# Linear attention and two MLPs: pass 4 takes blocks 1 to 8 in pairs, 512 columns wide, and VectorE turns the finished tiles

## The chip, the core and the metric

The kernel runs on 1 core of one Trainium2 chip. The metric is device time in microseconds (us), the median of several executions.

## What is computed

```python
kv = np.einsum('bhsd,bhse->bhde', k, v)              # batch 8, 8 heads, 576 tokens, head size 64
out = np.einsum('bhsd,bhde->bhse', q, kv)
rms = np.sqrt(np.mean(out * out, axis=-1, keepdims=True) + 1e-06)
x = out / rms * g_norm                               # then as 4608 tokens x 512
h = x @ w_in_1                                       # 512 x 2048
x = np.maximum(0.01 * h, h) @ w_out_1                # 2048 x 512
h = np.maximum(x @ w_in_2, 0.0)
out = (h * h) @ w_out_2                              # 4608 x 512, float32
```

## The kernel before, in words

The 4608 tokens are nine blocks of 512 (`TB`), and the two MLPs are four passes over them. Pass 1 computes attention and the first product with `w_in_1` (`gemm1`). Pass 2 multiplies with `w_out_1` (phase 0, `ph = 0`), pass 3 with `w_in_2` (`first`), pass 4 with `w_out_2` (`ph = 1`).

Every float32 operand of a matmul is split into a high and a low part (names ending in h and l), and three products hh, hl, lh are summed. ScalarE writes the high part (a copy to the rounded type), VectorE subtracts it and writes the low part.

Passes 2 to 4 multiply 2x2 blocks of matrices with seven products instead of eight, in Winograd's form (`PRODUCTS`): S1 to S4 are sums of quarters of the left operand A, T1 to T4 of the right operand B, and the products are added into the results C11, C22, C21 and C12. `ORDER` and `ORDER2` are the orders in which the products run. The 2048 values that are summed over come in four groups n of 512 (`NQ`), and within n in two halves c.

There are two ways to run a product with a `w_out`.

- `second_pass` and `second`: one block at a time, group by group and in it product by product, 256 columns wide. VectorE and ScalarE prepare the sums and the parts of the activations for each group (`prep`, `sum_op`, `hi_op`, `lo_op`). In phase 0 the weights are the left operand and the result stands with its features on the partitions. In phase 1 the activations are the left operand and the result stands with its tokens on the partitions, as `out` wants it.
- `pairs_pass` and `pair_second`: two blocks at a time, one the B11, B21 half and the other the B12, B22 half, product by product and in it group by group. A unit is one product and one group: 12 matmuls of 512 columns, weights on the left. `pair_load` loads a quarter (tile `dB`), `pair_sum` makes the T sums, `pair_hi` and `pair_lo` the parts (`dop_B..`, `dop_T..`; the digit in the name is the group n), and `adder` adds a finished PSUM tile (`dps`) to earlier sums into `du` or `do_C`.

Before the change pass 2 runs block 0 with `second_pass` and blocks 1 to 8 with `pairs_pass`; pass 4 runs all nine blocks with `second_pass`, in the order 7, 8, 0, 5, 6, 3, 4, 1, 2. So the weights of `w_out_1` are stored as A quarters and S sums, those of `w_out_2` as B quarters and T sums (`LEFT`).

The order of the work is written out as numbers: `at_slot(t, step)` puts a step at a place on a scale of slots, and the steps are emitted sorted by it. `tick` is called once for each product and group; a store that was put down by `store` is issued by SyncE (SP) two ticks later. All loads stand in the same SP queue, and a load waits there until the buffer it takes (46 of them, `NBIG`) is free. Weights come in 28 tiles, fetched as buffers come free; those of the second half are split on arrival (`split_loaded`). Finished tiles that wait for their store share 5 buffers (`hp`). PSUM's 8 banks are handed out in turn (`next_bank`), and `bank_swap` exchanges some at the start of pass 4, where the last products of pass 3 and the first of pass 4 alternate on TensorE.

Of the kernel before, what the change touches and what calls it, by code (L numbers as in the profile page):

```python
# [10 lines left out]
F32 = mybir.dt.float32  # L11
# [3 lines left out]
ALU = mybir.AluOpType  # L15
# [3 lines left out]
def tile_linear_attention_two_mlps(  # L19
# [111 lines left out]
    def pre_split(w, n):  # L131
# [3 lines left out]
         for j in range(NB if ph else 1)]  # L135
# [3 lines left out]
        j: [[dram.tile([P, 2, TB], F32, name=f"h{k}_{j}_{n}") for n in range(NQ)] for k in range(2)]  # L139
        for j in range(1, NB)  # L140
# [112 lines left out]
    LEFT = {(0, 1): 0, (1, 0): 0, (1, 1): 1}  # L253
# [16 lines left out]
    def store(out, in_, *slots):  # L270
        stores.append([out, in_, slots, 0])

    def tick():
# [14 lines left out]
    def sum_w2(w, n, name):  # L288
# [9 lines left out]
        w: [PRODUCTS[p][LEFT[w]] for p in (ORDER if w[0] else ORDER2)] for w in LEFT  # L298
# [429 lines left out]
    def operand(kind, b, name):  # L728
# [7 lines left out]
        if kind == 1:  # L736
            i, j = j, i
# [95 lines left out]
    def square(u, z, pairs, name):  # L833
# [22 lines left out]
    def second(ph, gg, x, free):  # L856
        j, n = gg
        tick()
        pr = (ORDER if ph else ORDER2)[x]
        if ph and n == 0 and pr == 1 and j == SETS[-1][0]:  # L860
            k = bank_n[0]
            bank_swap.update({(k + x) % 8: (k + y) % 8 for x, y in ((1, 2), (2, 3), (3, 1))})
# [3 lines left out]
        gname = PRODUCTS[pr][1 - ph]  # L866
        g = op_t[ph, gg, gname][0]
        last = n == NQ - 1
        for c in range(2):
            w = w2((ph, 1), 2 * n + c, x)  # L870
            for t in range(2):
                for y, (gh, wh) in enumerate(((0, 0), (0, 1), (1, 0))):
                    if ph == 0:
                        a, b = w[:, gh, t, :], g[wh][:, c, :]
                    else:
                        a, b = g[gh][:, c, t * P:(t + 1) * P], w[:, wh].rearrange("p c f -> p (c f)")
                    nc.tensor.matmul(  # L877
                        out=ps[:, t], lhsT=a, rhs=b,
# [11 lines left out]
        if pr == (1 if ph else 6):  # L890
# [6 lines left out]
        if pr in outs:  # L897
# [12 lines left out]
    d_done = set()  # L910
    PLACE = {"T3": "B12", "T2": "B11", "T4": "T3", "T1": "T2"}
# [417 lines left out]
```

## Time and profile before

| | |
|---|---|
| median of 3 runs | 1569.1 us (1567.08 to 1569.54) |
| the profiled execution | 1569.42 us, of which its span on the core 1567.6 us |
| TensorE busy | 1553.0 us, 9260 matmuls |
| VectorE, ScalarE busy | 1171.3 us, 808.1 us |
| granted TensorE clock | full in all slices |
| mean DMA rate | 202 GB/s |

The page gives the busy time of each engine (PE is TensorE's matmuls, PEld its weight loads, DVE VectorE, ACT ScalarE, SPq SyncE's queue of DMAs), the chain of work that ended last, the costliest groups of instructions and the DMAs. The trace is asked for parts of it: a timeline of an engine, busy times in stretches, the chain in order of time, one line's instructions. L877 is the matmul of `second`, L958 that of `pair_second`, L810 that of `first`, L789 is `adder`.

### The profile page before, as it was taken

What the parts mean: (1) busy time and instruction counts of PE and PEld (TensorE: products, weight loads), DVE (VectorE), ACT (ScalarE), POOL (GpSimd) and SP (SyncE); (2) the same over time, 40 slices, a digit from 0 to 9 for tenths busy, and PEclk for the clock granted to TensorE, in tenths of its full rate; (3) what the DMA queues carried; (4) which work ended last, traced back from release to release, by engine and by line L of the source; (5) the groups of instructions that cost most, each with busy time, mean ns of one, the idle gap of its engine ahead of it and who ended that gap; (6) DMA issues with size and microseconds to landing.
All of it is one profiled execution on the core that took longest, in us unless ns stands there. A gap on an engine that the chain in (4) does not pass through costs nothing.

```text
span 1567.6 us, 24422 instructions
## 1 busy us (share of the span) xinstructions
PE 1553.0 (99%) x9260; PEld 1357.0 (87%) x9260; DVE 1171.3 (75%) x1752; ACT 808.1 (52%) x1341; POOL 7.2 (0%) x16
## 2 busy tenths in 40 slices
PE   7999999999999999999999999999999999999999
PEld 5788888888888988888888888889888999999998
DVE  5866776777774988787776777767777887777776
ACT  5866666666665534344443544546446444443442
POOL 0000000000000000000000000000000000000000
PEclk9999999999999999999999999999999999999999
DMA  9978788889569737373746444655579444433332
GB/s 241 287 207 290 255 313 285 296 285 334 215 215 313 252 108 232 99 233 98 237 172 225 159 164 162 188 182 185 165 228 346 153 134 135 131 125 124 122 124 78
DMA packets 221525, 317.24 MB, mean 202 GB/s; under 512 B 52448, under 2 KB 150240, under 8 KB 221408
## 3 DMA queue, kind: packets, MB, share of 16 engines
q1 hardware_dynamic: 220048, 315.13, 61.7%
q8 instruction: 73, 1.20, 0.3%
q10 hardware_dynamic: 1360, 0.56, 0.1%
q14 instruction: 44, 0.36, 0.1%
HBM read 191.89 MB, written 123.73 MB: 201 GB/s over the span
## 4 chain that ended last, share of the span: by engine, by line
PE 97%; DMA 1%; DVE 1%; ACT 1%; issue 0%; SPq 0%; DVEq 0%
PE ps L877 25%; PE hps L675 25%; PE dps L958 19%; PE aps L810 12%; PE bps L810 9%; PE kvps L502 1%; PE qtps L554 1%; PE ops L581 1%; PE ops L580 1%; PE ops L579 1%; DMA w<-w 0%; PE ssps L609 0%; PE ssps L603 0%; DMA g<-h_C 0%; DMA v_raw<-in_v_dram 0%; PE ssps L601 0%
## 5 line engine op out<-in xcount | busy, mean ns | idle before, releaser
L675 PE MATMUL hps<-xh,w 128*128 128x512 f32 x1152 | 378.7, 396 | 2.1 <-ACT xh L632 1.3
L675 PEld LDWEIGHTS hps<-xh,w 128*128 128x128 f32 x1152 | 216.1, 188 | 49.8 <-DVE w L245 1.9
L675 PE MATMUL hps<-xl,w 128*128 128x512 f32 x576 | 224.6, 390 | 0.5 <-DVE xl L633 0.5
L675 PEld LDWEIGHTS hps<-xl,w 128*128 128x128 f32 x576 | 108.3, 188 | 22.7 <-issue 1.0
L687 ACT ACTIVATE h<-hps 128x512 f32<-128x512 f32 x144 | 85.0, 593 | 24.2 <-issue 10.2
L926 DVE TENSOR_TENSOR dB<-dB,dB 128x1024 f32<-128x1024 f32 x64 | 78.2, 1222 | 1.1 <-DMA dB<-h 0.2
L789 DVE TENSOR_TENSOR h_C<-aps,u 128x512 f32<-128x512 f32 x72 | 49.6, 688 | 38.8 <-PE aps L810 38.5
L789 DVE TENSOR_TENSOR u<-bps,p 128x512 f32<-128x512 f32 x72 | 49.5, 687 | 27.7 <-ACT p L820 17.9
L389 DVE TENSOR_TENSOR w<-w 128x512 fp32r<-128x512 f32 x56 | 37.8, 687 | 35.4 <-ACT w L388 35.4
L820 ACT ACTIVATE p<-aps 128x512 f32<-128x512 f32 x36 | 21.3, 592 | 74.9 <-PE aps L810 74.9
L562 DVE TENSOR_TENSOR qhl<-qtps,qhl 128x512 fp32r<-128x512 f32 x32 | 22.1, 691 | 46.2 <-ACT qhl L561 43.6
L810 PE MATMUL aps<-op_B21h,w 128*128 128x512 f32 (+1 forms) x160 | 51.8, 373 | 0.7 <-ACT p L820 0.7
L212 DVE SCALAR_TENSOR_TENSOR w_raw<-w_raw 128x512 uint32<-128x512 uint32 x64 | 44.1, 688 | 9.8 <-ACT w_raw L211 9.4
L810 PE MATMUL aps<-op_B22h,w 128*128 128x512 f32 (+1 forms) x160 | 51.1, 368 | 0.0
L810 PE MATMUL bps<-op_T4h,w 128*128 128x512 f32 (+1 forms) x160 | 51.1, 368 | 0.0
L810 PE MATMUL bps<-op_T3h,w 128*128 128x512 f32 (+1 forms) x160 | 51.0, 368 | 0.0
L810 PE MATMUL aps<-op_B11h,w 128*128 128x512 f32 (+1 forms) x160 | 51.0, 368 | 0.0
L810 PE MATMUL aps<-op_T1h,w 128*128 128x512 f32 (+1 forms) x160 | 51.0, 368 | 0.0
L810 PE MATMUL bps<-op_T2h,w 128*128 128x512 f32 (+1 forms) x160 | 51.0, 368 | 0.0
L620 DVE TENSOR_TENSOR sqo<-sqo,y 128x512 f32<-128x512 f32 x32 | 22.1, 692 | 35.2 <-ACT y L618 34.9
L827 ACT ACTIVATE h_C<-aps 128x512 f32<-128x512 f32 x36 | 21.5, 597 | 51.6 <-issue 32.9
L561 ACT ACTIVATE qhl<-qtps 128x512 fp32r<-128x512 f32 x32 | 19.1, 597 | 52.2 <-PE qtps L554 52.2
(908 smaller groups left out, 4032.9 us busy)
## 6 DMA issues: line engine op xcount, KB each, us to landing
g_raw<-g SPq DMA_DIRECT2D x80, 512.0 KB, 5.6
dB<-h SPq DMA_DIRECT2D x80, 512.0 KB, 4.0
g<-h_C SPq DMA_DIRECT2D x144, 256.0 KB, 2.4
h<-h SPq DMA_DIRECT2D x128, 256.0 KB, 4.6
w_raw<-in_moe_w_in_dram SPq DMA_DIRECT2D x32, 512.0 KB, 7.0
w_raw<-in_moe_w_out_dram SPq DMA_DIRECT2D x32, 512.0 KB, 6.8
x_raw<-x SPq DMA_DIRECT2D x32, 512.0 KB, 6.1
w<-w SPq DMA_DIRECT2D x56, 256.0 KB, 4.9
```

The costliest lines, as they stand in the source:

```text
L212: nc.vector.scalar_tensor_tensor(out=lower, in0=upper, scalar=0x80000000, in1=lower, op0=ALU.bitwise_and, op1=ALU.bitwise_or,)
L389: nc.vector.tensor_tensor(out=by_h[:, :, 1], in0=src[:, :, 1], in1=src[:, :, 0], op=ALU.subtract)
L562: nc.vector.tensor_tensor(out=t[:, 1], in0=ps, in1=f32(t[:, 0]), op=ALU.subtract)
L620: (nc.gpsimd if i == 1 else nc.vector).tensor_tensor(out=osb, in0=osb, in1=y, op=ALU.mult)
L675: nc.tensor.matmul(out=ps, lhsT=w[:, wh, c * P:(c + 1) * P], rhs=x_t[j][xh, c // 2][0][:, c % 2, :], start=(c == 0 and y == 0), stop=(c == ...
L687: nc.scalar.activation(out=h, in_=h_ps.pop((j, m)), func=AF.Prelu, alpha=0.01)
L789: nc.vector.tensor_tensor(out=t, in0=x, in1=y, op=ALU.add)
L810: nc.tensor.matmul(out=ps[:, p], lhsT=w[:, wh, c, :], rhs=t[xh][:, c, :], start=(fresh and p == 0 and c == 0 and y == 0), stop=(p == len(p ...
L827: nc.scalar.activation(out=h, in_=ps, func=AF.Relu)
L877: nc.tensor.matmul(out=ps[:, t], lhsT=a, rhs=b, start=(n == 0 and c == 0 and t == 0 and y == 0), stop=(last and c == 1 and y == 2), skip_g ...
L926: nc.vector.tensor_tensor(out=to[0], in0=d_t[z, x, n][0], in1=d_t[z, y, n][0], op=op)
L958: nc.tensor.matmul(out=ps[t], lhsT=w[:, wh, t, :], rhs=ops[gh][:, c, :], start=(n == 0 and at == pr and c == 0 and y == 0), stop=(last and ...
```

## The change

- Pass 4 runs block 0 with `second_pass` and then the pairs (7, 8), (5, 6), (3, 4), (1, 2) with `pairs_pass`, as pass 2 does; the functions of the pairs get the phase as an argument. The weights of `w_out_2` are prepared as A quarters and S sums.
- Pass 3 stores the blocks 1 to 8 in the layout that the pairs load (`h_d[1, ...]`).
- The results of pass 4 now stand with their features on the partitions. VectorE turns each finished tile in 32x32 blocks (`turned`), and `store_out` writes a turned tile in 4 DMAs, one for each 32 features, whose runs in `out` are 32 floats. For C11 of a pair the transpose reads PSUM and takes the place of ScalarE's copy. The last two tiles' DMAs are issued by SP and ScalarE in turn.
- In the last group of each product of a pair, in both passes, the first half of the tile (`t = 0`) is finished before the second.
- The first two steps of pass 3 stand 2.5 slots earlier, and `bank_swap` at the start of pass 4 exchanges two triples of banks.

The diff, without the renaming of keys and arguments in the pair functions:

```diff
-    LEFT = {(0, 1): 0, (1, 0): 0, (1, 1): 1}
+    LEFT = {(0, 1): 0, (1, 0): 0, (1, 1): 0}
...
-            store(
-                g_d[1][SETS[z][t]][n][:, i, :, cp * U:(cp + 1) * U],
-                h.rearrange("p c (t u) -> p (c t) u", t=2),
-            )
+            store(h_d[1, SETS[z][t]][i][n][:, cp], h.rearrange("p c t -> p (c t)"))
...
-        pr = (ORDER if ph else ORDER2)[x]
-        if ph and n == 0 and pr == 1 and j == SETS[-1][0]:
+        pr = ORDER2[x]
+        if ph and n == 0 and pr == 6:
             k = bank_n[0]
-            bank_swap.update({(k + x) % 8: (k + y) % 8 for x, y in ((1, 2), (2, 3), (3, 1))})
+            bank_swap.update({(k + x) % 8: (k + y) % 8 for x, y in ((1, 2), (2, 3), (3, 1), (4, 5), (5, 6), (6, 4))})
...
             if ph == 0:
-                to = x2_d[j][2 * i:2 * i + 2].rearrange("c p t -> p c t")[:, :, o * U:(o + 1) * U]
+                store(x2_d[j][2 * i:2 * i + 2].rearrange("c p t -> p c t")[:, :, o * U:(o + 1) * U], e)
             else:
-                t0 = j * TB + i * U
-                to = out[t0:t0 + U, o * U:(o + 1) * U].rearrange("(c p) f -> p c f", p=P)
-            store(to, e)
+                et = turned(f"t{j}_{name}", e)
+                for t in range(2):
+                    store_out(j * TB + o * U, 2 * i + t, et[:, t], U)
+
+    R = 32
+
+    def turned(name, src):
+        t = hp.tile(list(src.shape), F32, tag="h", name=name)
+        flat = (lambda x: x) if len(src.shape) == 2 else lambda x: x.rearrange("p c t -> p (c t)")
+        nc.vector.transpose(flat(t), flat(src))
+        return t
+
+    def store_out(t0, f, t, n, last=False):
+        for b in range(P // R):
+            f0 = f * P + b * R
+            store(
+                out[t0:t0 + n, f0:f0 + R].rearrange("(c r) f -> r c f", r=R),
+                t[b * R:(b + 1) * R].rearrange("r (c f) -> r c f", f=R),
+                by=nc.scalar if last and b % 2 else nc.sync,
+            )
...
-        for c in range(2):
-            w = w2((0, 1), 2 * n + c, x)
-            for t in range(2):
-                for y, (wh, gh) in enumerate(((0, 0), (0, 1), (1, 0))):
+        ws = [w2((ph, 1), 2 * n + c, x) for c in range(2)]
+        for c, t in sorted(((c, t) for c in range(2) for t in range(2)), key=lambda ct: ct[1] if last else ct[0]):
+            for y, (wh, gh) in enumerate(((0, 0), (0, 1), (1, 0))):
...
-                if pr == 2:
+                if pr == 2 and ph:
+                    e = ps[t]
+                elif pr == 2:
...
-                store(x2_d[SETS[z][o]][2 * i + t], e)
+                if ph:
+                    et = turned(f"dt{z}_{name}{t}", e)
+                    store_out(SETS[z][o] * TB, 2 * i + t, et, TB, pr == 3 and z == Z_ORDER[1][-1])
+                else:
+                    store(x2_d[SETS[z][o]][2 * i + t], e)
...
-                    at_slot(at0, "f", u, z, mine, n, free)
+                    at_slot(at0 if u or n > 1 else at0 - 2.5, "f", u, z, mine, n, free)
...
-        second_pass(t3, 1, [j for half, z in insts if half for j in SETS[z]])
+        pairs_pass(second_pass(t3, 1, [0]), 1)
```

Three places in the order of the program show it. On TensorE, after the first block of pass 4 (`ps_7`, `ps_8` are PSUM tiles of blocks 7 and 8, the digit behind them the product; `w_11` are tiles of the weights), there stood before:

```order
L877 MATMUL ps_7_3_11424<-w_11_24_11416,op_(7, 3)_S_11678 128x256 x6
L877 MATMUL ps_7_3_11424<-w_11_27_11471,op_(7, 3)_S_11678 128x256 x6
L877 MATMUL ps_8_6_11840<-w_11_0_10834,op_(8, 0)_S_11702 128x256 x6
L877 MATMUL ps_8_6_11840<-w_11_3_10905,op_(8, 0)_S_11702 128x256 x6
L877 MATMUL ps_8_1_11857<-w_11_0_10834,op_(8, 0)_A_11716 128x256 x6
L877 MATMUL ps_8_1_11857<-w_11_4_10928,op_(8, 0)_A_11716 128x256 x6
```

and now, after block 0:

```order
L870 MATMUL ps_0_4_11433<-op_(0, 3)_T_11695,w_11_23_11420 128x256 x6
L870 MATMUL ps_0_4_11433<-op_(0, 3)_T_11695,w_11_27_11503 128x256 x6
L870 MATMUL ps_0_3_11456<-op_(0, 3)_B_11726,w_11_24_11448 128x256 x6
L870 MATMUL ps_0_3_11456<-op_(0, 3)_B_11726,w_11_27_11503 128x256 x6
L968 MATMUL dps_1_0_11897<-dop_B_0h,w_11_0_10866 128x512
L968 MATMUL dps_1_0_11897<-dop_B_0l,w_11_0_10866 128x512
```

The next block's groups of 256 columns gave way to the pair's units of 512.

On VectorE, where a block of pass 4 ends (`o_C` and `do_C` are finished tiles, `sS` sums, `op` and `dop` operands), there stood before:

```order
L789 TENSOR_TENSOR o_C_14722<-ps_4_2_14350,p_14_14701 128x512
L769 TENSOR_TENSOR op_(1, 0)_A_14705<-g_raw_1_0_1_14553,op_(1, 0)_A_14705 128x512
L789 TENSOR_TENSOR u_14_14739<-ps_4_7_14366,u_14_14703 128x512
L769 TENSOR_TENSOR op_(1, 0)_S_14725<-sS_1_(1, 0)_14708,op_(1, 0)_S_14725 128x512
L769 TENSOR_TENSOR op_(1, 0)_S_14741<-sS_1_(1, 0)_14664,op_(1, 0)_S_14741 128x512
L789 TENSOR_TENSOR u_14_14758<-ps_4_5_14383,u_14_14703 128x512
L789 TENSOR_TENSOR o_C_14760<-ps_4_5_14383,u_14_14739 128x512
```

and now, from C21 of the pair (7, 8) to the first operands of the pair (5, 6):

```order
L789 TENSOR_TENSOR do_C_12380<-dps_4_0_12302,du_140_12124 128x512
L906 STREAM_TRANSPOSE dt_C_12382<-do_C_12380 128x512
L789 TENSOR_TENSOR do_C_12384<-dps_4_1_12303,du_141_12126 128x512
L906 STREAM_TRANSPOSE dt_C_12386<-do_C_12384 128x512
L952 TENSOR_TENSOR dop_B_2l<-dB_14_2_12132,dop_B_2h 128x1024
L937 TENSOR_TENSOR dB_13_2_12230<-dB_13_2_12320,dB_13_2_12230 128x1024
L952 TENSOR_TENSOR dop_B_3l<-dB_14_3_12151,dop_B_3h 128x1024
```

The transposes stand between the adders and the next low parts.

On SP, in the second pair of pass 4, the stores of a C (here C22) now stand between the loads of the next pair's quarter B22 (`dB22_12`), 8 DMAs in a row:

```order
L931 DMA dB22_12_2_12906<-h1_1_4_2_235 128x1024
L281 DMA out_0_dram<-dt3_C220_12876 32x16x32 x4
L281 DMA out_0_dram<-dt3_C221_12880 32x16x32 x4
L931 DMA dB22_12_3_12933<-h1_1_4_3_236 128x1024
L931 DMA dB11_12_0_12952<-h1_0_3_0_221 128x1024
```

Before, a C of pass 4 left in one DMA.

## Rows read from the trace of the kernel before

**Rows 1.** The page, part 1: busy us (share of the span) xinstructions

```profile
PE 1553.0 (99%) x9260; PEld 1357.0 (87%) x9260; DVE 1171.3 (75%) x1752; ACT 808.1 (52%) x1341; POOL 7.2 (0%) x16
```

**Rows 2.** The chain in order of time, its long pieces: start us, us, what

```profile
506.85 40.46 PE ps L877 x336
547.31 304.67 PE dps L958 x1344
...
1208.12 355.68 PE ps L877 x2964
```

**Rows 3.** Stretches, a pair and a block: us, busy by engine, PEclk, DMA share, GB/s

```profile
699.50:775.60 76.10, 76.10 (x337) 63.06 (x336) 58.51 (x55) 32.23 (x33) 0.00 (x0) 1.00 0.52 166
1251.00:1291.30 40.30, 40.30 (x338) 40.30 (x337) 33.35 (x54) 16.97 (x30) 0.00 (x0) 1.00 0.43 145
```

**Rows 4.** TensorE's timeline at two seams: start us, us, what [idle before <-releaser]

```profile
855.53 0.38 PE L810 MATMUL aps<-op_B21h,w 128*128 128x256 f32 x1 [0.69 <-ACT p L820]
...
1205.03 1.70 PE L877 MATMUL ps<-w,op_(7, 0)_S 128*128 128x256 f32 x12 [1.24 <-DVE h_C L789]
```

**Rows 5.** The timeline of VectorE and TensorE in pass 4's first block

```profile
1226.36 0.69 DVE L389 TENSOR_TENSOR w<-w 128x512 fp32r<-128x512 f32 x1 [1.28 <-ACT w L388]
1226.96 0.69 DVE L769 TENSOR_TENSOR op_(7, 3)_S<-sS_(7, 3)_11577,op_(7, 3)_S 128x512 fp32r<-128x512 f32 x1
...
1241.07 1.60 PE L877 MATMUL ps<-w,op_(8, 0)_S 128*128 128x256 f32 x12
```

**Rows 6.** The page, part 5, VectorE: xcount | busy us, mean ns | idle before

```profile
L926 DVE TENSOR_TENSOR dB<-dB,dB 128x1024 f32<-128x1024 f32 x64 | 78.2, 1222 | 1.1 <-DMA dB<-h 0.2
...
L389 DVE TENSOR_TENSOR w<-w 128x512 fp32r<-128x512 f32 x56 | 37.8, 687 | 35.4 <-ACT w L388 35.4
```

**Rows 7.** Line 591, a one-source copy: ns min/median/max, first and last start us

```profile
L591 DVE CAST sqs<-sqo x28: 419/426/429, 86.7 to 447.2; 128x512 fp32r<-128x512 f32 x28
```

**Rows 8.** VectorE's timeline at two seams between pairs of pass 2

```profile
699.01 1.37 DVE L789 TENSOR_TENSOR do_C<-dps,du 128x512 f32<-128x512 f32 x2 [0.18 <-PE dps L958]
700.30 1.22 DVE L941 TENSOR_TENSOR dop_B_2l<-dB,dop_B_2h 128x1024 fp32r<-128x1024 f32 x1
...
759.60 1.23 DVE L941 TENSOR_TENSOR dop_B_0l<-dB,dop_B_0h 128x1024 fp32r<-128x1024 f32 x1 [1.33 <-PE dps L958]
...
764.34 1.32 DVE L789 TENSOR_TENSOR do_C<-dps,du 128x512 f32<-128x512 f32 x2
...
767.85 1.22 DVE L941 TENSOR_TENSOR dop_B_3l<-dB,dop_B_3h 128x1024 fp32r<-128x1024 f32 x1
768.98 1.22 DVE L926 TENSOR_TENSOR dB<-dB,dB 128x1024 f32<-128x1024 f32 x1
```

**Rows 9.** TensorE's timeline behind the first of these seams

```profile
704.93 0.39 PE L958 MATMUL dps<-dop_B_2h,w 128*128 128x512 f32 x1
...
707.65 0.39 PE L958 MATMUL dps<-dop_B_3h,w 128*128 128x512 f32 x1
```

**Rows 10.** DMA queues, 20 to 60 us: packets, MB, share of 16 engines

```profile
DMA packets 16165, 10.51 MB, mean 263 GB/s; under 512 B 5993, under 2 KB 16161, under 8 KB 16161
...
q1 hardware_dynamic: 16161, 10.46, 109.1%
```

**Rows 11.** DMA queues, 1240 to 1540 us

```profile
q1 hardware_dynamic: 17179, 39.68, 40.2%
```

**Rows 12.** SP's timeline at the second seam: stores of C22, then loads

```profile
756.99 0.86 SPq L279 DMA_DIRECT2D x<-do_C  x2
759.33 7.81 SPq L920 DMA_DIRECT2D dB<-h  x4
```

**Rows 13.** Loads of q, tile q_raw: issue ns min/median/max, first and last start

```profile
L542 SPq DMA_DIRECT2D q_raw<-in_q_dram x126: 533/598/1675, 0.7 to 390.4; - x126
```

**Rows 14.** The page, part 6: xcount, KB each, us to landing

```profile
dB<-h SPq DMA_DIRECT2D x80, 512.0 KB, 4.0
```

**Rows 15.** The chain's last piece: start us, us, what

```profile
1563.83 0.69 DVE o_C L789
```

More of the change, by code (lines that the diff above doesn't have):

```diff
@@ L134, in tile_linear_attention_two_mlps @@
         [[dram.tile([P, 2, 2, TB], F32, name=f"g{ph}_{j}_{n}") for n in range(NQ)]
-         for j in range(NB if ph else 1)]
+         for j in range(1)]
         for ph in range(2)
@@ L138, in tile_linear_attention_two_mlps @@
     h_d = {
-        j: [[dram.tile([P, 2, TB], F32, name=f"h{k}_{j}_{n}") for n in range(NQ)] for k in range(2)]
-        for j in range(1, NB)
+        (ph, j): [
+            [dram.tile([P, 2, TB], F32, name=f"h{ph}_{k}_{j}_{n}") for n in range(NQ)] for k in range(2)
+        ]
+        for ph in range(2) for j in range(1, NB)
     }
@@ L268, in tile_linear_attention_two_mlps, with store @@
     stores = []
-    def store(out, in_, *slots):
-        stores.append([out, in_, slots, 0])
+    def store(out, in_, *slots, by=nc.sync):
+        stores.append([out, in_, slots, 0, by])
     def tick():
@@ L277, in tick @@
         while stores and stores[0][3] > 1:
-            to, src, slots, _ = stores.pop(0)
-            nc.sync.dma_start(out=to, in_=src)
+            to, src, slots, _, by = stores.pop(0)
+            by.dma_start(out=to, in_=src)
             give_big(*slots)
@@ L297, in tile_linear_attention_two_mlps @@
     w_names = {
-        w: [PRODUCTS[p][LEFT[w]] for p in (ORDER if w[0] else ORDER2)] for w in LEFT
+        w: [PRODUCTS[p][LEFT[w]] for p in (ORDER2 if w[1] else ORDER)] for w in LEFT
     }
@@ L872, in second @@
                 for y, (gh, wh) in enumerate(((0, 0), (0, 1), (1, 0))):
[L873 to L876, printed above, removed]
                     nc.tensor.matmul(
-                        out=ps[:, t], lhsT=a, rhs=b,
+                        out=ps[:, t], lhsT=w[:, gh, t, :], rhs=g[wh][:, c, :],
                         start=(n == 0 and c == 0 and t == 0 and y == 0),
@@ L889, in second @@
             u_t["p1"] = p1
-        if pr == (1 if ph else 6):
+        if pr == 6:
             u_t["u2"] = adder("gl", f"u2_{ph}{j}", bank[6], u_t["p1"])
@@ L910, in tile_linear_attention_two_mlps @@
     d_done = set()
+    Z_ORDER = (list(range(1, len(SETS))), list(range(len(SETS) - 1, 0, -1)))
     PLACE = {"T3": "B12", "T2": "B11", "T4": "T3", "T1": "T2"}
@@ L1109, in second_pass @@
             gs = [(j, n) for j in blocks for n in range(NQ)]
-            steps = prep("TS"[ph], not ph)
+            steps = prep("T", True)
             for x, gg in enumerate(gs):
@@ L1121, in second_pass, with pairs_pass @@
                     at_slot(at0 + n + 0.1, "s2", ph, gg, n, True)
-                if ph and gg[0] == blocks[-1]:
-                    at_slot(at0 + NPR, "wd", (ph, 1), gg[1])
             return t0 + NPR * len(gs)
         at_slot(0, "lag", 5)
-        def pairs_pass(t0):
-            for z in range(1, len(SETS)):
+        def pairs_pass(t0, ph):
+            for z in Z_ORDER[ph]:
                 def at_unit(w, *st):
```

92 lines of the change are left out of this document (46 added, 46 removed).

## The prediction

> **What bounds the kernel now.** I read the page's first part, then the chain of work that ended last in order of time, then the busy time of the engines stretch by stretch. TensorE is busy 1553.0 of 1567.6 us [rows 1], so only what shortens or interrupts its own stream counts. The chain shows the stages in that stream [rows 2]: block 0 of pass 2, 336 matmuls 256 columns wide in 40.46 us, 120.4 ns each; the pairs of pass 2, 1344 matmuls 512 wide in 304.67 us, 226.7 ns each; pass 4 without its first dozens of matmuls, 2964 matmuls 256 wide in 355.68 us, 120.0 ns each. A column costs 0.469 ns in pass 4 and 0.443 ns in the pairs. The stretches say why [rows 3]: in a block of pass 4 the weight loads are busy 40.30 of 40.30 us, so each 256-column product waits for its load; in a pair they are busy 63.06 of 76.10 us, and the 512 columns cover them. Pass 4 is bound by weight loads and pass 2's pairs are not.
>
> **Matmuls.** Pass 4 now runs 9 x 336 = 3024 matmuls of 256 columns. After, block 0 keeps its 336, and 2688 of 256 become 1344 of 512: 2688 x 120.0 ns = 322.6 us against the 304.67 us which the same program of four pairs took in pass 2: **-17.9 us**. All of it lies on TensorE, which sets the end. The exchange of A sums for B sums in the weights of pass 4 keeps the number and size of the operations of pass 1: nothing. So does the new layout of pass 3's stores: the same bytes in half the packets, beside pass 3's matmuls.
>
> **The seams.** Between pass 3 and pass 4 TensorE waits 1.24 us, for a VectorE adder that empties a PSUM bank [rows 4]. After, product 5 goes to the bank of an older, already emptied tile and that bank to product 3, two to three products later: -1.24 us, if nothing else is late. Between passes 2 and 3 TensorE waits 0.69 us for ScalarE's copy of product 1 [rows 4], because product 2 follows on the same bank. The two still stand side by side after the change; only product 6 has moved: nothing.
>
> Something else is late: VectorE at the first pair. No earlier row shows this mix, so I add up the new order from the last split of weights, which starts at 1226.36; the next operation starts at 1226.96 [rows 5]. From there to the end of the low part of B11's third quarter stand 18 operations of 512 elements and 7 of 1024; they follow each other every 0.60 and 1.13 us [rows 5, 8]: 18.7 us, so 1245.7. TensorE wants it two units of 2.72 us after the start of the pair: at 1246.5 with today's start of 1241.07 [rows 5], at 1245.3 if the 1.24 us are gained. So most of that gain is handed back: **+1.0 us**, with bounds of 0 and 3.5 (VectorE today idles 1.4 us in that stretch, and two more units hang on it).
>
> **VectorE.** A pair takes it 58.5 of 76.1 us [rows 3]. The trace has no 32x32 transpose. Nearest rows: for 512 elements a one-source copy takes 426 ns [rows 7] and a two-source operation 687 ns, and one of 1024 elements, as if each element passed twice, 1222 ns [rows 6]. I take 0.69, as for all other work on this shape; 8 of them bring a pair to 64.0 of 76.1 us. Their place matters more. Where a pair ends, VectorE works from 759.60 on without a gap [rows 8], and the transposes of C21 (2) and C12 (2) fall there. C22's two, 1.2 us, are taken up by the gap of 1.33 us before that. C21's push the rest back by 1.2 us: the adders of C12, free at 699.01 - 0.18 = 698.83 now, start at 700.0, four operations take 2.4 us, and the low part of B11's third quarter ends at 703.7. TensorE wants it at 704.93 and the fourth at 707.65 [rows 9]: 1.2 us of slack, today 3.4. So 0.69 us costs **nothing** and 1.22 us would cost 0.9 us at each of three seams.
>
> **DMA and SP.** A finished tile of 128 x 512 leaves in 4 DMAs of 64 KB, 2048 packets of 128 B in all; a pair has 8 tiles, so 16384 packets, 1024 for each of the 16 DMA engines. The trace has no such packet. Two stretches give the price of mean sizes: 1.091 x 16 x 40 us / 16161 = 43.2 ns at 647 B [rows 10], 0.402 x 16 x 300 us / 17179 = 112.3 ns at 2310 B [rows 11]. The line through both gives 21.6 ns at 128 B, my estimate; bounds are 8.5 (in proportion to bytes) and 43.2 (a packet costs what it cost at 647 B). A pair of pass 2 keeps the engines busy 0.52 of the time [rows 3], 39.6 us; less 64 packets of 2 KB for the x stores (101 ns each by the line, 6.5 us) and plus 1024 x 21.6 ns it is 55 of 76.1 us: it fits. SP issues 2 stores per quarter of a result now, in 0.86 us [rows 12], and 8 after; loads of up to 512 packets take it 598 ns each [rows 13], so 4.8 us. Behind the stores of C22 waits the fourth load of B22. It now leaves at 759.33, after at 757.0 + 4.8 = 761.8, and with the 4.0 us of such loads [rows 14] lands at 765.8, behind the burst (256 packets per engine, 5.5 us) perhaps at 767; the sum that needs it starts at 768.98 [rows 8]. Behind C21's stores waits the fourth load of B11, with more room. A new wait: C21's second adder takes the buffer of C22's first turned tile and needs its four DMAs landed: 757.0 + 4 x 0.6 + 4.0 = 763.4, against 764.34 and two operations of 0.6 [rows 8], 765.5. All of this is covered: **nothing**, and cover of 2 us is thin.
>
> **The tail.** Now the last adder ends at 1563.83 + 0.69 = 1564.52 [rows 15], 3.1 us before the span's end. After, the first half tile ends 1.36 us earlier and keeps VectorE until the last adder; that one needs a transpose (0.69) and the second of two issues on its queue (0.6), and 8 DMAs, 256 packets per engine, must pass: by the chain of the second half +1.5 us, by the packets at 21.6 ns about +3. I take **+2.5**, bounds +1.5 and +8.5 (43 ns).
>
> **Sum.** The profiled execution took 1569.42 us, span 1567.6, 0.3 above the median of 1569.1. 1569.4 - 17.9 - 1.2 + 1.0 + 2.5 = **1553.8 us**; its own range is 1551.5 to 1558.
>
> **Rivals.** A: a transpose takes about 1.2 us. Then 0.9 us at each of three seams, 4 x 0.53 + 1.4 at the first pair, 1 in the tail: 1561. For it speaks that VectorE has no gap at the seams; against it, that every row of 512 elements is at 0.43 or 0.69. The Trainium skill (VectorE: DVE Perf Modes, The three transpose paths) gives VectorE 311 ns for a 128x128 bf16 transpose; four of them would be 1.24 us, an estimate, and with that the sum is this rival's. No row here shows one.
>
> B: a packet costs 30 to 43 ns. A burst then keeps the queues 8 to 11 us, the loads behind it land after 768.98, VectorE waits and passes it on; at 43 ns the queues are busy 77 of 76.1 us in a pair, 1.8 us per pair counting one late load, and the tail takes 6 more: 1558 to 1567, say 1563.
>
> C, the other side: the output's small writes become the bound. A pair then takes 33.1 + 1.024 t us with t in ns per packet. Against the net gain of 15.6, 3.9 per pair, it decides from t = 46 ns; at 60 ns a pair takes 94.5 us and with the tail the kernel 1637 us. Against it: 5993 of the packets of [rows 10] are under 512 B, and the mean there is still 43.2 ns. For it: those were reads, and no row has a write to DRAM under 512 B. The Trainium skill (DMA: Bandwidth & Descriptors, Specifications) asks for 512 B per transfer and says that below this the engine reads, modifies and writes. If that meant two passes of 21.6 ns the case would be B's upper end, if it meant more, C.
>
> That the change doesn't do what it says is next to nothing: the order of TensorE shows the pairs, and their speed is measured in pass 2.
>
> **How the numbers follow.** Forecast 0.58, A 0.13, B 0.13, C 0.12; 0.04 for the rest, half below 1551, half between 1567 and 1572. The range 1551 to 1567 leaves out C and the rest, 0.16. About 0.2% (3.1 us) is what a measurement of this kernel can tell from no change, so faster is below 1566: 0.58 + 0.13 + 0.11 + 0.02 = 0.84; same 0.04; slower 0.12.
>
> **What would show it.** The chain should have a piece of 1344 matmuls of about 304.7 us in pass 4 as well as in pass 2, and a weight-load share of 83% there. The transposes should be near 0.69 us, 36 of them (32 of pairs, 4 of block 0), and TensorE's waits in pass 4 no more than 1 to 3 us, the first at the third unit of the first pair. The DMA share in a pair should be near 0.73; above 0.95 B or C holds. The tail from the last matmul to the end should be near 6.5 us. The forecast is wrong if TensorE waits several microseconds at each seam, and what it waits for (a low part behind transposes, or behind a load) tells A from B.

## The result, and the profile after

The change makes the kernel faster: 1554.95 us (median; 1554.27 to 1555.79) against 1568.44 us for the kernel before on the same chip, a ratio of 0.9914 with a 95% interval of 0.9902 to 0.9927. The prediction was 1553.8 us, in a range of 1551 to 1567. The profiled execution took 1554.27 us, its span 1552.5 us.

The page, part 1, answers to [rows 1]; the long pieces of the chain (start us, us, what) to [rows 2]; the stretch of the second pair of pass 4 to the first row of [rows 3]:

```profile
PE 1536.8 (99%) x7916; PEld 1286.3 (83%) x7916; DVE 1170.2 (75%) x1596; ACT 797.5 (51%) x1229; POOL 7.2 (0%) x16
```

```profile
1206.03 27.37 PE ps L870 x228
...
1249.14 296.70 PE dps L968 x1307
```

```profile
1316.10:1392.50 76.40, 76.40 (x339) 63.26 (x338) 63.65 (x64) 30.61 (x30) 0.00 (x0) 1.00 0.61 165
```

TensorE is still the bound, with 1344 matmuls less. A pair of pass 4 runs as one of pass 2 does: no wait in it, the weight loads busy 83%. TensorE's waits from pass 3 on (engine, line <- what it waited for: us in total, times, longest) answer to [rows 4]:

```profile
PE bps L810 <- DVE u L789: 0.9, 1, 0.9
...
PE dps L968 <- DVE dop_B_2l L952: 0.7, 1, 0.7
PE aps L810 <- ACT p L820: 0.7, 1, 0.7
PE dps L968 <- DVE dop_B_3l L952: 0.6, 1, 0.6
```

The 1.24 us for VectorE's adder between passes 3 and 4 are gone, the 0.69 us for ScalarE's copy are as before, the first pair has two waits, as forecast, and one wait is new: 0.9 us in pass 3, at 862 us.

**Where two executions may be compared.** The end of pass 1 (the last start of line 677, in the kernel before line 675) wanders by itself; before first, after behind it:

```profile
L675 PE MATMUL hps<-xh,w x1152: 387/389/793, 28.4 to 506.5; 128*128 128x512 f32 x192
```

```profile
L677 PE MATMUL hps<-xh,w x1152: 387/389/793, 28.7 to 504.9; 128*128 128x512 f32 x192
```

In the twelve kernels below, which all do the same up to there, it lies between 504.7 and 508.2 us. From there on the stretches that kernels have in common mostly repeat to 0.2 us. So I compare stretches behind it: from the end of pass 1 to the end of the span the kernel before takes 1567.6 - 506.5 = 1061.1 us and the changed one 1552.5 - 504.9 = 1047.6: -13.5 us, the same as the medians give. The 15.1 us between the two spans hold 1.6 us of that wandering.

### The profile page after: what moved, and what is told of

Its sections match the earlier page's. It is cut to its first block, busy times and chain, and to the rows that moved or that the text cites. A ratio compares the mean times of both kernels' runs of the same rounds, so it can differ in the third digit from the quotient of the medians.

```text
span 1552.5 us, 21563 instructions
## 1 busy us (share of the span) xinstructions
PE 1536.8 (99%) x7916; PEld 1286.3 (83%) x7916; DVE 1170.2 (75%) x1596; ACT 797.5 (51%) x1229; POOL 7.2 (0%) x16
## 5 line engine op out<-in xcount | busy, mean ns | idle before, releaser
L937 DVE TENSOR_TENSOR dB<-dB,dB 128x1024 f32<-128x1024 f32 x128 | 156.1, 1220 | 1.9
L968 PE MATMUL dps<-dop_T_3h,w 128*128 128x512 f32 x256 | 84.0, 389 | 0.0
L968 PE MATMUL dps<-dop_T_2h,w 128*128 128x512 f32 x256 | 84.0, 389 | 0.0
L968 PE MATMUL dps<-dop_T_0h,w 128*128 128x512 f32 x256 | 84.0, 389 | 0.0
L968 PE MATMUL dps<-dop_T_1h,w 128*128 128x512 f32 x256 | 84.0, 389 | 0.0
L968 PE MATMUL dps<-dop_B_2h,w 128*128 128x512 f32 x192 | 63.1, 389 | 0.0
L968 PE MATMUL dps<-dop_B_3h,w 128*128 128x512 f32 x192 | 63.1, 389 | 0.0
L968 PE MATMUL dps<-dop_B_0h,w 128*128 128x512 f32 x192 | 63.0, 389 | 0.0
L968 PE MATMUL dps<-dop_B_1h,w 128*128 128x512 f32 x192 | 63.0, 389 | 0.0
L968 PEld LDWEIGHTS dps<-dop_T_1h,w 128*128 128x128 f32 x256 | 48.1, 188 | 10.0
```

The lines of the kernel that those rows point to most:

```text
L937: nc.vector.tensor_tensor(out=to[0], in0=d_t[ph, z, x, n][0], in1=d_t[ph, z, y, n][0], op=op)
L968: nc.tensor.matmul(out=ps[t], lhsT=ws[c][:, wh, t, :], rhs=ops[gh][:, c, :], start=(n == 0 and at == pr and c == 0 and y == 0), stop=(last ...
```

## The experiments

### Why 512 columns are cheaper

```diff
-                nc.tensor.matmul(
-                    out=ps[t], lhsT=ws[c][:, wh, t, :], rhs=ops[gh][:, c, :],
+                for cols in (slice(0, 320), slice(320, TB)) if ph else (slice(0, TB),):
+                    nc.tensor.matmul(
+                        out=ps[t][:, cols], lhsT=ws[c][:, wh, t, :], rhs=ops[gh][:, c, cols],
```

(That is e10_uneven; e2_split2 has two slices of 256 columns, e1_split4 four of 128. In all three the start mark of a sum is set on each narrow product, so the results are not those of the computation above; number, size and order of the instructions are as told.)

> In the pairs of pass 4 each matmul of 512 columns is issued as two of 256 with the same weights (2688 instead of 1344 there), all else as in the changed kernel. If width is all that the 17.9 us of the matmul term came from, it goes away: 2 x 120.0 - 226.7 = 13.3 ns x 1344 = +17.9 us, 1572.8 us, by both readings of e1_split4. Rival: the layout (weights on the left, two blocks at a time) brings something of its own, or weights that are used twice in a row come cheaper; then less than +17.9 us, 1555 to 1570.

> In the pairs of pass 4 each matmul of 512 columns is issued as four of 128 with the same weights (5376 instead of 1344 there). Two readings of why 512 columns are cheaper by the column than 256 are told apart. L (my prediction's words, a 256-column product waits for its weight load): a narrower product waits just as long, 120.0 ns, so four take 480 ns instead of 226.7, 1344 x 253 ns = +340 us, 1895 us; if weights that stand already are not loaded again, the number of loads stays at 1344 and the time goes up much less. F (each matmul costs a fixed part): 120.0 = a + 256 b and 226.7 = a + 512 b give a = 13.3 ns and b = 0.417 ns, so 128 columns take 66.7 ns, four 266.7, 1344 x 40 ns = +53.8 us, 1608.7 us. Both give the same for 256 and 512 columns, so the result so far does not tell them apart.

> In the pairs of pass 4 each matmul of 512 columns is issued as one of 320 and one of 192 with the same weights. e1_split4 gave 111.5 ns for 128 columns; 256 take 120.0 and 512 take 226.7. M (the longer of a floor of 111.5 ns set by the weight load and 13.3 ns + 0.417 ns a column): 146.7 + 111.5 = 258.2 ns instead of 226.7, x 1344 = +42.3 us, 1597.3 us. L (my prediction: products of 256 columns and fewer wait for a load of 120 ns): 146.7 + 120.0 = 266.7 ns, +53.7 us, 1608.7 us. D (loads run more than one ahead and only their sum counts, 223 ns for two, under the 240.0 ns of the columns): +17.9 us, 1572.8 us.

Measured: 1573.0, 1849.1 and 1597.5 us, one execution each. One stretch of 100 us inside the pairs, of e1_split4, e2_split2 and e10_uneven in this order (columns as in [rows 3]; the first bracket is the number of matmuls):

```profile
1400.00:1500.00 100.00, 100.00 (x898) 100.00 (x897) 37.12 (x36) 20.14 (x20) 0.00 (x0) 1.00 0.23 66
```

```profile
1400.00:1500.00 100.00, 100.00 (x836) 100.00 (x834) 78.38 (x77) 37.44 (x38) 0.00 (x0) 1.00 0.60 160
```

```profile
1400.00:1500.00 100.00, 100.00 (x776) 100.00 (x775) 77.26 (x76) 36.02 (x35) 0.00 (x0) 1.00 0.59 155
```

That is 111.4 ns for 128 columns, 119.6 for 256, and 257.7 for a product of 320 and one of 192 together. Weights that are used twice in a row are loaded twice: the second bracket, the loads, counts as many as the first. e2_split2 gives the 17.9 us back: an undisturbed unit takes 2.88 us from start to start instead of 2.72, and a pass has 112 of them. That its time meets the expected 1572.8 so closely is in part chance: counted from the end of pass 1 it takes 17.1 us more than the changed kernel, and loses 0.5 less at the first pair. So width alone made the matmul term. e1_split4 fits neither reading: F gave 66.7 ns, L 120.0. Out of both came M, the longer of a floor of 111.4 ns and 13.3 ns + 0.417 ns a column; e10_uneven was the test and came out at 1597.5 where M gave 1597.3, L 1608.7 and D 1572.8. So a matmul of 256 columns does not wait for its load, though the loads are busy all the time next to it [rows 3]: it pays a fixed 13.3 ns, as one of 512 does, and doubling the width saves one of two of these. The floor would bind under (111.4 - 13.3) / 0.417 = 235 columns, an estimate from these figures. That it is the load which sets the floor is argued, since no run changed the load alone. The Trainium skill (TensorE: Matmul & The Clock Gate, LDWEIGHTS (loading the stationary operand)) gives a load its columns divided by 1.2 in ns, 107 ns for 128; the 111.4 ns agree within 5%.

### What the transposes cost, and what they nearly cost

The rows of line 906 (ns min/median/max, first and last start) answer the open price, which I had taken between [rows 6] and [rows 7]:

```profile
L906 DVE STREAM_TRANSPOSE dt_C<-do_C x24: 711/711/712, 1295.3 to 1546.6; 128x512 f32<-128x512 f32 x24
...
L906 DVE STREAM_TRANSPOSE dt_C<-dps x8: 708/716/717, 1283.8 to 1513.2; 128x512 f32<-128x512 f32 x8
L906 DVE STREAM_TRANSPOSE t_C<-o_C x4: 711/711/712, 1239.3 to 1247.3; 128x512 f32<-128x512 f32 x4
```

The Trainium skill (VectorE: DVE Perf Modes, The three transpose paths) led to an estimate of 1.24 us; these rows have 0.71. First the transposes and the small stores were taken out of the pairs, then each transpose was doubled, then those of C22 alone:

```diff
-                    et = turned(f"dt{z}_{name}{t}", e)
-                    store_out(SETS[z][o] * TB, 2 * i + t, et, TB, pr == 3 and z == Z_ORDER[1][-1])
+                    r0 = SETS[z][o] * TB + (2 * i + t) * P
+                    store(out[r0:r0 + P, :], e)
```

> The pairs of pass 4 store their tiles unturned, in one DMA of 2 KB runs per tile (the output is not in order; ScalarE copies C11 as in pass 2). Theory: transposes and small writes cost only in the tail, 6.7 us from the last matmul now against 3.8 us before the change, so -2.9 us, 1552.0 us; VectorE in a pair falls from 63.7 by 8 x 0.65 to 58.5 us. The DMA share of a pair falls from 0.61: at 13.6 ns a packet of 128 B (the tail's mean) 1024 of them are 13.9 us, 64 packets of 2 KB take 6.5, so to 0.51; at the 21.6 ns of my prediction it would fall to 0.41. Rival: the small writes slow the matmuls themselves or the loads, then more than 3 us comes back, and the piece of matmuls in the chain gets shorter by the matmul.

Measured: 1552.04 us, ratio 0.9894 (0.9878 to 0.9911). From pass 4's second product (the first of a T sum, at 1197.3 us in the changed kernel) to the start of the last matmul it takes 347.9 us against 348.1 in the changed kernel; from there to the end 2.9 us less. The second pair:

```profile
1316.20:1392.50 76.30, 76.30 (x338) 63.19 (x337) 58.56 (x55) 31.50 (x32) 0.00 (x0) 1.00 0.51 166
```

VectorE 58.6 us and DMA 0.51, as expected, so transposes and small writes cost nothing but the tail.

```diff
-        nc.vector.transpose(flat(t), flat(src))
+        for _ in range(2):
+            nc.vector.transpose(flat(t), flat(src))
```

> Every transpose is done twice in a row into the same tile (72 instead of 36). My theory of rival A's price: VectorE has only 0.28 us to spare at the third unit of a pair (low part of B11's third quarter ends at 1322.48, TensorE takes it at 1322.76), so of the four more transposes of C21 and C12 at 0.64 us each (2.6 us) 2.3 us come out at each of three seams, 6.9 us; at the first pair, where VectorE is already late, four more cost 2.6 us; the tail 1.3 us. Sum +10.8 us: 1565.7 us, with TensorE waiting about 2.3 us at the third and fourth unit of the second to fourth pair. Rival: VectorE idles 17% of a pair, so it takes them up, and only the tail shows: +1.3 us, 1556.2 us.

Measured: 1577.43 us, ratio 1.0056 (1.0041 to 1.0071), 22 us over the changed kernel where I expected 10.8: slower than before the change. TensorE waits twice at each seam, not once, for the third unit of product C12 and for that of the next pair's first product:

```profile
1319.65 0.50 PE L969 MATMUL dps<-dop_B_2l,w 128*128 128x512 f32 x1 [2.40 <-DVE dop_B_2l L953]
...
1333.11 0.50 PE L969 MATMUL dps<-dop_B_2l,w 128*128 128x512 f32 x1 [2.29 <-DVE dop_B_2l L953]
```

A pair takes 81.86 us instead of 76.19: 5.7 us more, and 8 x 0.71 us are 5.7. All of the additional work comes out, though VectorE idles 17% of a pair of the changed kernel. My sum had let C22's part be taken up by the idle time behind it.

> Only the transposes of C22 in the pairs are done twice: 8 more in all, 2 for each pair. My prediction had the two transposes of C22 taken up by VectorE's idle time of 1.1 to 1.3 us behind them; if a gap there is free time, 1.37 us more is taken up too, or nearly, and the time is 1555.0 to 1555.3 us. Rival, from e3_turn2 (there nearly all of 8 x 0.69 us came out at each seam): that idle time is VectorE waiting for ScalarE's high part, which in turn waits for VectorE's low part (2.35 us a unit), so it moves along and takes up nothing; then the spare time at the last product (0.28 us) is gone and 1.37 - 0.28 = 1.1 us comes out in each of three seams, +3.3 us: 1558.3 us.

Measured: 1559.08 us, ratio 0.9937 (0.9920 to 0.9953). This is the rival's side, and a little beyond: pass 4 takes 352.3 us to its last matmul, +4.2, which is 3 x 1.4 and so all of the 2 x 0.71 us. TensorE's list of waits shows less than that, 0.8 us at each of the three seams:

```profile
PE dps L969 <- DVE dop_B_2l L953: 3.1, 4, 0.8
```

(The fourth is the first pair's, as in the changed kernel.) From start to start such a unit loses 1.1 us, and the third unit of C12 before it loses 0.3 without a wait in the list. The idle time of 1.13 us that VectorE shows before each low part ends with ScalarE's high part:

```profile
1297.17 1.23 DVE L953 TENSOR_TENSOR dop_T_0l<-dB,dop_T_0h 128x1024 fp32r<-128x1024 f32 x1 [1.13 <-ACT dop_T_0h L947]
```

```profile
1296.08 1.06 ACT L947 ACTIVATE dop_T_0h<-dB 128x1024 fp32r<-128x1024 f32 x1 [1.29 <-DVE dop_T_3l L953]
1298.43 1.06 ACT L947 ACTIVATE dop_T_1h<-dB 128x1024 fp32r<-128x1024 f32 x1 [1.29 <-DVE dop_T_0l L953]
```

(VectorE, then ScalarE, in e3_turn2; [idle before <-releaser].) Each high part waits for the low part before it and each low part for its high part, 2.35 us a unit: VectorE idles because it is in a chain, and work put in moves the chain.

### Smaller writes

The tiles still get turned, but leave in rows of their own, in 4 DMAs whose runs are 8 floats (e7_run32) or 4 (e8_run16):

```diff
+                    for b in range(4):
+                        store(
+                            out[r0:r0 + P, :].rearrange("p (x b f) -> p x b f", b=4, f=8)[:, :, b],
+                            et.rearrange("p (x b f) -> p x b f", b=4, f=8)[:, :, b],
```

> Each turned tile of the pairs of pass 4 leaves in 4 DMAs whose runs are 8 floats (32 B) instead of 32, in rows of their own (the output is not in order): 65536 packets in a pair instead of 16384. The DMA share of a pair without the small stores is 0.61 x 76.4 - 13.9 = 32.7 us. By the line through 13.6 ns at 128 B (tail of the changed kernel) and 43.2 ns at 647 B [rows 10] a 32 B packet takes 8.1 ns: 4096 x 8.1 = 33 us, share 0.86, and the time stays within some 5 us of 1555 (as rival B: late loads behind the stores). If a packet never falls under 13.6 ns: 56 + 33 = 89 us in a pair, +12 us each, 1603 us. If a write under a limit of size costs extra: more.

> As e7_run32 with runs of 4 floats (16 B): 131072 packets in a pair, 8192 for each DMA engine. This is past the point of rival C, however it comes out: by the line 7.2 ns a packet, 59 + 32.7 = 92 us in a pair instead of 76.3, +15.4 us each, and 2 x 16384 packets in the tail, 15 us: 1630 us. If a packet never falls under 13.6 ns: 144 us in a pair, 1840 us. If the price goes by bytes alone, the time stays at 1555 us. Rival C's rule (a pair takes 33 us plus its packets when that is over 76 us) holds if the pair's time is 33 us plus 8192 times the price that the DMA rows give.

Measured: 1625.5 and 2320.2 us, one execution each. The issues on SP of the tiles' stores (ns min/median/max) in the changed kernel, e7_run32 and e8_run16:

```profile
L281 SPq DMA_DIRECT2D out_dram<-dt_C x124: 315/503/1969, 1287.5 to 1549.4; - x124
```

```profile
L281 SPq DMA_DIRECT2D out_dram<-dt_C x124: 533/1386/6023, 1288.0 to 1615.7; - x124
...
  DVE dt_C L906: 15.7, 8
```

```profile
L281 SPq DMA_DIRECT2D out_dram<-dt_C x124: 540/6850/14736, 1289.2 to 2298.0; - x124
...
  DVE dt_C L906: 301.8, 12
```

The price of a 32 B packet came out near the line's 8.1 ns. A stretch of e7_run32 that holds a pair's 336 matmuls (columns as in [rows 3]), and its packets:

```profile
1431.50:1523.00 91.50, 81.98 (x336) 65.42 (x334) 61.55 (x60) 30.45 (x30) 0.00 (x0) 0.94 0.74 137
```

```profile
DMA packets 64797, 12.51 MB, mean 137 GB/s; under 512 B 62233, under 2 KB 62233, under 8 KB 64793
...
q1 hardware_dynamic: 64793, 12.45, 73.7%
```

0.737 x 91.5 - 32.7 = 34.7 us for 62233 / 16 = 3890 packets of an engine, 8.9 ns. Yet the kernel lost 70.6 us, with the DMA engines busy 74% only. Pass 4 to its last matmul is 58.2 us longer, and the tail 12.4. TensorE's listed waits in the pairs are 36 us; and in this stretch its granted clock is 0.94, and it was busy 82.0 us with 336 matmuls, which take 76.2 at full clock. The same sum over the four pairs gives 22 us, the rest of the 58.2. The waits go back to what I had called covered: a store holds SP for 1.4 us instead of 0.5, the loads behind it go out late, and VectorE waits for one of the 5 buffers of finished tiles (15.7 us, 8 times; in the changed kernel never). SP at one group of stores, and ScalarE's wait for loads in the pairs:

```profile
1302.98 14.34 SPq L281 DMA_DIRECT2D out_dram<-dt_C  x8
```

```profile
ACT dop_B_0h L946 <- DMA dB<-h: 47.5, 3, 16.9
```

Once issued, such a load lands after 4.9 us instead of 4.1, so most of the delay is SP's.

At 16 B the price jumps. Between 1500 and 2000 us of e8_run16 (packets, MB, share of 16 engines):

```profile
q1 hardware_dynamic: 247565, 23.27, 123.0%
```

16 x 500 us / 247565 = 32.3 ns a packet by the wall (the loads among them), over three times the 32 B one for half the bytes, and a share over 1 says that packets' times overlap. All three of my prices were wrong for it. From the third unit of one pair to that of the next it takes 270 us, which is what all its packets take at this price; rival C's rule, 33 + 8192 x 0.0323 = 298 us, counts the loads twice. So the jump on which rival C rested exists, but between 32 and 16 B: at 128 and 32 B the price lies far below the 43.2 ns of [rows 10]. The Trainium skill (DMA: Bandwidth & Descriptors, Specifications) sets the limit under which a write is read, modified and written at 512 B; no run here shows one there. The changed kernel's 128 B packets take 13.6 ns: in its last 6.5 us 4224 of them (123 B on average) make a share of 27.8% + 27.6%, 0.554 x 16 x 6.5 us / 4224.

### The seams and the tail

```diff
-            bank_swap.update({(k + x) % 8: (k + y) % 8 for x, y in ((1, 2), (2, 3), (3, 1), (4, 5), (5, 6), (6, 4))})
+            bank_swap.update({(k + x) % 8: (k + y) % 8 for x, y in ((1, 2), (2, 3), (3, 1))})
```

> The second triple of the exchange of banks at the start of pass 4 is taken out; all else as in the changed kernel. By my prediction the 1.24 us wait at the seam of passes 3 and 4 returns, but most of it was handed back at the first pair, where VectorE works without a gap and its low part of B11's third quarter does not come earlier: so the waits only trade places (1.2 us at the seam, 1.27 us at the first pair shrinking to under 0.3), and the time stays at 1555.0 us, within 0.4. Rival: both waits stand, +1.2 us, 1556.2 us.

Measured: 1556.16 us, ratio 0.9922 (0.9908 to 0.9937). The median is the rival's, the trace is not: the wait is back at the seam,

```profile
PE ps L870 <- DVE h_C L789: 1.3, 1, 1.3
```

both waits of the first pair are gone from the list (its fourth unit still loses 0.3 us from start to start), and from pass 4's second product to the last matmul it takes 348.1 us, to the tenth what the changed kernel takes. Pass 1 ended 3.3 us later in this execution, which is the wandering of the start. So the banks bring nothing as long as VectorE is late at the first pair.

```diff
-                    at_slot(at0 if u or n > 1 else at0 - 2.5, "f", u, z, mine, n, free)
+                    at_slot(at0, "f", u, z, mine, n, free)
```

> The first two steps of pass 3 stand where they stood before the change; all else as in the changed kernel. The changed kernel has a wait that the kernel before has not, 0.89 us of TensorE for VectorE's adder u at 862 us, and keeps the 0.69 us wait for ScalarE's copy of product 1. Theory: with the two steps earlier, VectorE's u stands in front of the sum that used to fill its idle time (1.37 us idle before u, the sum after it), so everything behind comes 1.2 us late; undone, the 0.89 us goes away and the 0.69 us stays: 1554.1 us. Rival: the wait has another cause (the half by half order of the pairs of pass 2), then it stays: 1555.0 us.

Measured: 1554.92 us, ratio 0.9915 (0.9898 to 0.9931). The 0.9 us wait is gone and the 0.7 us one stays; from the first product T1 of pass 3 to pass 4's second product it takes 338.0 us against 339.0. In the medians 1 us does not show.

```diff
-        for c, t in sorted(((c, t) for c in range(2) for t in range(2)), key=lambda ct: ct[1] if last else ct[0]):
+        for c, t in sorted(((c, t) for c in range(2) for t in range(2)), key=lambda ct: ct[0]):
```

> In the last group of a product the matmuls of a pair run in the old order again (half c by half c) in both passes. In the tail the first half tile is then finished 0.68 us before the last matmul instead of 1.36: its adder and transpose (1.34 us) keep VectorE until 0.66 us after it, the second half's adder starts 0.6 us later and the tail grows from 6.7 to 7.3 us. At the seams VectorE has work queued in front of the adders, so nothing there: +0.6 us, 1555.6 us. Rival: the adders of C21 and C12 start later too, and with 0.28 us to spare there TensorE waits 0.4 us at each of three seams: +1.8 us, 1556.8 us.

Measured: 1557.33 us, ratio 0.9923 (0.9908 to 0.9938). From the last matmul to the end it takes 7.3 us instead of 6.7, as expected. At the seams of pass 4 the list has no wait, but from start to start the third unit of the second, third and fourth pair takes 2.91 us instead of 2.72; TensorE at the first of them:

```profile
1325.00 0.39 PE L968 MATMUL dps<-dop_B_2h,w 128*128 128x512 f32 x1
...
1327.91 0.39 PE L968 MATMUL dps<-dop_B_3h,w 128*128 128x512 f32 x1
```

That is 0.2 us at each of three seams: the rival's mechanism is there, at half its price. The profiled span is 3.6 us longer. Of the other 3.0 us, 1.8 are a later end of pass 1, and 0.7 lie in pass 2, with a listed wait of 0.4 us for a low part in block 0, which runs ahead of the pairs and which the edit does not touch; 0.4 are pass 4's.

Last, a kernel with the three costs of the change taken away:

```diff
+                    at_slot(at0, "f", u, z, mine, n, free)
...
...
-                et = turned(f"t{j}_{name}", e)
...
+                late_turns.append((j, name, i, o, e))
...
+        for x in range(4):
+            at_slot(t4 + 2 * (4 + x) - 5.4 + 0.035, "lt")
...
-                by=nc.scalar if last and b % 2 else nc.sync,
+                by=nc.sync,
```

(`t4` is the slot at which the pairs of pass 4 begin; "lt" turns and stores the next of block 0's four tiles.)

> The changed kernel with its three costs taken away: the first two steps of pass 3 where they stood (0.89 us, as in e6_f_back); the four transposes of block 0 done at units 4 to 7 of the first pair instead of between its low parts (the 1.27 us of waits there); and all of the last 8 DMAs issued by SP, since in the tail SP's second issue stands from 1546.29 to 1548.51 behind a DMA of ScalarE's queue, and the last one is out at 1549.93, while four in a row from 1547.33 at 0.45 us each are out at 1549.2 (0.7 us). Theory: the three add up, -2.9 us, 1552.1 us; the distance from the first product of pass 4 to the last matmul falls from 348.1 to 346.8 us. Rival: VectorE is late anyway in the first pair, further on, and the 1.27 us comes back at T products: 1553.4 us.

Measured: 1552.86 us, ratio 0.9894 (0.9879 to 0.9909), 4 executions. From the end of pass 1 to the end of the span it takes 1549.4 - 504.7 = 1044.7 us, 2.9 us less than the changed kernel; the two intervals against the kernel before still overlap a little. By place: 1.0 us in pass 3, 1.9 us in pass 4 (346.2 us; more than expected), and nothing in the tail: eight DMAs at 0.50 us each in one queue end as late as four and four with the stall. The chain of pass 4's pairs is now one piece:

```profile
1237.84 304.75 PE dps L974 x1344
```

1344 matmuls in 304.75 us, where pass 2 has 304.67 [rows 2]. From the start of the first to the start of the last matmul of the pairs it takes 304.5 us (1237.68 to 1542.19) and in the changed kernel 306.5 (1238.98 to 1545.44), 1.9 us more: that is the true price of the first pair. The listed waits (1.27 us) understate it. They count from the modelled end of the matmul before, 0.39 us after its start, while undisturbed ones follow each other after 0.227; and the matmuls right behind a wait follow each other more slowly, the first of them after 0.33 us. Each makes up 0.3 us for the two waits.

## Why the prediction was right, point by point

**Matmuls, -17.9.** Right in size: 304.75 us against 304.67 once nothing disturbs. Both widths had been measured in the kernel before, so the size did not hang on the reason. Wrong in its reason: I read "busy 40.30 of 40.30 us" as the weight loads being the bound. They are next to it (the floor is 111.4 of 120.0 ns), and the saving is the fixed 13.3 ns of 1344 matmuls, 17.9 us. A busy share of 100% did not tell which of two things that overlap ends last; a change of width did.

**Seam of passes 3 and 4, -1.2; first pair, +1.0.** The first is right; the second came out at 1.9, inside its bounds of 0 and 3.5. The row that the sum went for, the low part of B11's third quarter, I had ending at 1245.7, and TensorE waits for it where forecast; VectorE's rows and TensorE's answer to [rows 5]:

```profile
1244.31 1.18 DVE L952 TENSOR_TENSOR dop_B_2l<-dB,dop_B_2h 128x1024 fp32r<-128x1024 f32 x1
...
1247.90 1.18 DVE L952 TENSOR_TENSOR dop_B_3l<-dB,dop_B_3h 128x1024 fp32r<-128x1024 f32 x1
```

```profile
1245.55 0.50 PE L968 MATMUL dps<-dop_B_2l,w 128*128 128x512 f32 x1 [0.72 <-DVE dop_B_2l L952]
...
1249.14 0.50 PE L968 MATMUL dps<-dop_B_3l,w 128*128 128x512 f32 x1 [0.55 <-DVE dop_B_3l L952]
```

It ends at 1245.49. That the two times agree is luck: the pair begins at 1238.98 and not at the 1239.83 that the sum went by, and behind that start the low part ends after 6.5 us where the sum gave 5.9. The 18 and 7 operations took 19.3 us, not 18.7. And the +1.0 left out the wait at the fourth unit, behind C12's transpose, which only the bounds allowed for.

**Seam of passes 2 and 3, "nothing changes".** Wrong by 1 us. The 0.69 us is where it was, but the two steps that moved took VectorE's adder u with them, in front of a sum that used to fill its wait for ScalarE; the sum came late, and the next u with it. VectorE before, then after:

```profile
852.62 1.22 DVE L749 TENSOR_TENSOR sT<-x_raw,x_raw 128x1024 f32<-128x1024 f32 x1
855.51 0.69 DVE L789 TENSOR_TENSOR u<-bps,p 128x512 f32<-128x512 f32 x1 [1.67 <-ACT p L820]
```

```profile
853.84 0.69 DVE L789 TENSOR_TENSOR u<-bps,p 128x512 f32<-128x512 f32 x1 [1.37 <-ACT p L820]
854.45 1.22 DVE L749 TENSOR_TENSOR sT<-x_raw,x_raw 128x1024 f32<-128x1024 f32 x1
```

The next u starts 6.36 us behind this one before the change and 7.63 after. With the two steps moved back (e6_f_back) it is 6.36 again and the wait is gone. I had looked at which product follows on which bank, and not at what stands behind u on VectorE.

**Transposes at 0.69, nothing at the seams.** 0.71, 63.65 us in a pair where I had 64.0, and nothing at the seams. But the slack was read wrongly. I had 1.2 us at the end of a pair; it is 0.28 us (VectorE above, TensorE below, at the last units of one product and of the next), where [rows 8, 9] had seemed to leave more:

```profile
1309.33 1.18 DVE L952 TENSOR_TENSOR dop_B_2l<-dB,dop_B_2h 128x1024 fp32r<-128x1024 f32 x1
...
1321.30 1.18 DVE L952 TENSOR_TENSOR dop_B_2l<-dB,dop_B_2h 128x1024 fp32r<-128x1024 f32 x1
```

```profile
1311.87 0.39 PE L968 MATMUL dps<-dop_B_2l,w 128*128 128x512 f32 x1
...
1322.76 0.40 PE L968 MATMUL dps<-dop_B_2l,w 128*128 128x512 f32 x1
```

1.36 us ahead at the first place, 0.28 at the second: here four units hold 11.97 us of VectorE's work, and TensorE takes 10.89 for them. The step that failed is "C22's two are taken up by the gap of 1.33 us": e11_turn2_c22 showed that this gap takes up nothing. So rival A, at about 1.2 us a transpose, was underpriced: by the measure of e3_turn2, where all of the additional work came out, 8 x 0.5 us, about 4 us at each of three seams (an estimate) and not 0.9.

**DMA and SP, nothing.** Right, with room: a packet takes 13.6 ns and not 21.6, the share of a pair is 0.61 and not 0.73, SP's issue takes 0.50 us where I had 0.6 from [rows 12, 13], and VectorE never waits for a tile's buffer. e7_run32 shows what the cover was worth: with issues of 1.4 us the same two waits that I named come out. Rival B's mechanism, late loads behind the stores, was right, but by what the stores take from SP's queue and not by the busy share, which is 0.74 in that kernel's pair.

**Tail, +2.5.** It is 6.66 us from the last matmul where it was 3.8 [rows 15]: +2.9. Part of the reason was another. SP's four issues in the tail:

```profile
1545.97 0.32 SPq L281 DMA_DIRECT2D out_dram<-dt_C  x1
1548.51 0.32 SPq L281 DMA_DIRECT2D out_dram<-dt_C  x1
1548.93 0.45 SPq L281 DMA_DIRECT2D out_dram<-dt_C  x1
1549.42 0.51 SPq L281 DMA_DIRECT2D out_dram<-dt_C  x1
```

SP's second issue stands for 2.2 us with its data ready. What it waits for is not shown. The landing of the first DMA that ScalarE issued, at 1545.97 too, would fit (those of its queue land 1.8 to 2.5 us after their issue), but no run here tells it apart, since e9_better changed the queue and found the issue rate instead.

The sum by the traces, from the end of pass 1: -17.9 - 1.4 (the seam, counted from start to start as the pair is) + 1.9 + 1.0 (the new wait, likewise) + 2.9 = -13.5, and -13.5 were measured. The forecast was -15.6: 0.9 us too little for the first pair, 1.0 for the wait not seen, 0.4 in the tail, less 0.2 at the seam.

## What to carry to other kernels

An idle share is spare time only if the engine could have worked then: where two engines hand each other every step, follow the chain unit by unit and count how far it is ahead at each place, since doubling 0.7 us of "covered" work here cost all of it. When a step moves earlier, look at what stands behind its instructions on every engine that they pass. Compare executions over stretches behind the part that wanders, not by their ends, and from start to start: the list of waits leaves out part of what a wait costs, and small waits altogether.

## What the runs showed of the hardware that I had not expected

- At full clock a matmul of these pairs costs the longer of 111.4 ns and 13.3 ns + 0.417 ns a column, from 128 to 512 columns (e1_split4, e2_split2, e10_uneven).
- Writes of 128 B and 32 B to DRAM take 13.6 and 8.9 ns of an engine, and with writes of 16 B a packet takes 32.3 ns by the wall (the changed kernel, e7_run32, e8_run16). The issuing engine feels it too: 0.50, 1.39 and 6.85 us for a DMA of 512, 2048 and 4096 packets.
- Where TensorE waited much, its granted clock was lower too: with TensorE busy 82.0 of 91.5 us the mean was 0.94 (e7_run32), with 61 of 200 us it was 0.63, between the levels of 2.4 and 1.2 GHz (e8_run16). Behind one wait of 24.8 us it was 0.50, the lower level, and matmuls of 512 columns followed each other after 0.43 us instead of 0.227:

```profile
1300.00:1500.00 200.00, 61.05 (x206) 46.66 (x205) 39.20 (x38) 18.82 (x20) 0.00 (x0) 0.63 1.34 38
1449.90:1454.70 4.80, 4.77 (x11) 3.51 (x11) 1.23 (x1) 0.00 (x0) 0.00 (x0) 0.50 1.68 13
```
